# Two attentions on one core: new costs in the plan for Pool, and a copy three steps later

## The chip, the cores and the metric

The kernel runs on one core of a Trainium2 chip. The engines are PE (matrix products), DVE (vector), ACT (activations), POOL (GpSimd) and SP, which issues nearly all DMAs. The metric is the device time of one execution, in microseconds (us), as the median of several runs.

## The reference

For one input `x` (2048 rows of 448 values, 16 heads of 28) two attentions are computed and mixed by a gate.

```python
x = A_x
g = _sigmoid((x * gate_w).sum(-1, keepdims=True))
a = _A_ref(x, A_wqkv, A_wo)
b = _B_ref(x, B_wqkv, B_wo)
return g * a + (1 - g) * b
```

A is a local attention: each row looks at itself and at the seven rows 2, 4, ... 14 places before it, with a softmax over these eight. B is full attention of every row to all 2048. Each has its own projection to queries, keys and values and its own output projection.

## The kernel before

**Stages.** First PE projects `x` to all queries, keys and values (about 250 us). Then come 16 *units* (`NU`), one for each group of four heads and block of 512 queries, each of 16 *steps* (one tile of 128 keys). A step `st` is numbered `16 * unit + tile`, so step 85 is unit 5, tile 5. Last, PE applies the output weights, partly inside units 14 and 15.

**A step.** In `scores` PE makes the score tiles of four heads (three matmuls each, L1022), ACT takes their exponentials (L1025), and PE multiplies the tile before with the values into the bank `av` (L976). Between them PE does up to three matmuls (L144) for the *row maxima* of the unit after the next: DVE reduces these banks to `MX` (L148) and PE needs the banks back. Every 21 or 22 steps one unit's maxima are complete: `max_parts` has ACT write `nmt` and `nmv` (L179, L180) and Pool subtract them (L181, `nmt`); two steps later DVE transposes the result (L186, `nms`) and SP stores it.

**What follows a unit.** While the next unit runs, the result of the last is normalised. `f` is the first step of the next unit, and a tuple gives the steps after it: `fin_copy` (ACT, `osb<-av`, L831) at step 1, `fin_sum` and `fin_sum2` (SP, the row sums out and in again as `fsum`), `fin_inv` (DVE reciprocal L844, Pool `finv` L845), `fin_spread` and `fin_spread2` (SP, `rs<-finv` L849, `rbc<-rs` L854), `fin_on` (Pool, `on<-osb,rbc`, L883), `fin_hi` (ACT, `onhi<-on`, L887), `fin_lo` (Pool, `onlo`, L891), `fin_store` (SP, eight DMAs of 56 KB to `on_hi` and `on_lo`). There is one `osb`.

**Local attention.** It runs on Pool and DVE beside the units, in 8 chunks of channels. For each chunk Pool has eight products of scores (L611, some followed by a half sum, L616), the softmax (L627, L634, L649, L650), eight products with the values (L661) and seven sums (L666); DVE reduces (L621, L632, L642). A planner places them: `item` puts every piece with a cost in us into a list for its engine, and `issue` takes from it, step by step, what is ready by the plan, until the engine's planned lateness `late` would go over a limit (4.2 for Pool). After each step `late` falls by the step's length, 2.25. Work that isn't in the list is added to `late` by hand (`pool_time`). The plan decides in which step's place a piece is written; the engines then run their queues in the order written, and wait only for data. When the lists are empty, `a_done` loads and splits the output weights, with a shift `d` that depends on the step.

Of the kernel before, what the change touches and what calls it, by code (L numbers as in the profile page):

```python
# [20 lines left out]
NU = NG * NB  # L21
# [4 lines left out]
def gated_mix_kernel(ctx: ExitStack, tc: tile.TileContext, xT, xn, gw, wA, wB, woAB, out):  # L26
    nc = tc.nc
# [156 lines left out]
    def max_turn(t):  # L184
        r = sp.tile([128, 32], F32, name="nms")
        nc.vector.transpose(r, t)  # L186
        return r
# [18 lines left out]
    with tc.tile_pool(name="xp", bufs=1) as xp, tc.tile_pool(name="wp", bufs=2) as wp:  # L206
# [203 lines left out]
        r, t = xst[:, 0, 0:3, :], xst[:, 0, 3, :]  # L410
# [40 lines left out]
        for n, t in enumerate(tiles):  # L451
# [4 lines left out]
            for w in splits:  # L456
                i, k = (n - splits[w][0]) * splits[w][1], splits[w][1]
# [36 lines left out]
            if parts and parts[0][0] <= n:  # L494
                _, u, t = parts.pop(0)
                max_store(u, max_turn(t.bitcast(F32)))
            if finished and n < len(tiles) - 3:
                u = finished.pop(0)
# [10 lines left out]
            if n == 70:  # L509
                r = max_turn(omw)  # L510
# [10 lines left out]
    def at(pos, st, f):  # L521
        hooks.setdefault((st, pos), []).append(f)
# [12 lines left out]
    pool = ctx.enter_context(tc.tile_pool(name="psv", bufs=1, space=bass.MemoryType.PSUM))  # L535
# [55 lines left out]
    for nme in ("k", "v"):  # L591
        for i in range(2):
            t = a1.tile([128, HALO + NJ, 56], F32, name=f"{nme}t{i}")
# [3 lines left out]
    def a_load(c, nme):  # L597
        if nme == "q":
            qt[c] = a2.tile([128, NJ, 56], F32, name="qt")
            nc.sync.dma_start(qt[c], a_own[0][c])  # L600
        else:
            t = kvt[nme, c % 2]
            i = 1 if nme == "k" else 2
            nc.sync.dma_start(t[:, 0:HALO, :], a_prev[i][c, :, NJ - HALO:NJ, :])
            nc.sync.dma_start(t[:, HALO:, :], a_own[i][c])

    def a_score(c, w):
        if w == 0:
            Lt[c] = a2.tile([128, W, NJ, 2], F32, name="L", bufs=3)
        p = a3.tile([128, NJ, 56], F32, tag="prod", name="prod")  # L610
        nc.gpsimd.tensor_tensor(out=p, in0=qt[c], in1=kvt["k", c % 2][:, HALO - DIL * w:HALO - DIL * w + NJ, :],  # L611
                                op=ALU.mult)
        prods[c, w] = p.rearrange("p j (h d) -> p (j h) d", d=DH)
        if NR[c, w] == 2:
            lo, hi = prods[c, w][:, :, 0:DH // 2], prods[c, w][:, :, DH // 2:]
            nc.gpsimd.tensor_tensor(out=lo, in0=lo, in1=hi, op=ALU.add)  # L616
            prods[c, w] = lo

    def a_reduce(c, w, i, n):
        r = slice(2 * NJ // n * i, 2 * NJ // n * (i + 1))  # L620
        nc.vector.tensor_reduce(Lt[c][:, w].rearrange("p j h -> p (j h)")[:, r], prods[c, w][:, r], axis=X, op=ALU.add)  # L621
# [56 lines left out]
    def item(eng, key, name, cost, needs, f):  # L678
        lists[eng].append((key, name, cost, needs, f))

    CH, NR = 21, {}
# [4 lines left out]
    for c in range(8):  # L686
        c0 = CH * c
        for nme in "qkv":
            item("sp", c0 if nme != "v" else c0 + 18, ("ld", nme, c), 0,
                 [(("s", c - 2, 7), 3)] if nme != "v" else [(("a", c - 2, 7, 1), 3)],  # L690
                 lambda c=c, nme=nme: a_load(c, nme))
        for w, o in enumerate((0, 2, 5, 8, 11, 14, 17, 20)):
            back = (c, w - 4) if w > 3 else (c - 1, w + 4)
            item("pool", c0 + o, ("s", c, w), 2.05 + 1.0 * (NR[c, w] == 2),
                 [(("ld", "k", c), 4), (("ld", "q", c), 4), (("a", c - 3, 7, 0), 0), (("s", c, w - 1), 0)]
                 + ([(last(*back), 0)] if back in NR else []), lambda c=c, w=w: a_score(c, w))
            for i in range(NR[c, w]):
                item("dve", c0 + o + 2 + 0.1 * i, ("r", c, w, i), 0.32,
                     [(("s", c, w), 3), (("r", c, w, i - 1) if i else last(c, w - 1) if w else ("r",), 0)],
                     lambda c=c, w=w, i=i: a_reduce(c, w, i, NR[c, w]))  # L700
        for i, (eng, o, cost, lag) in enumerate((("pool", 22, 0.68, 2), ("dve", 23, 0.35, 3), ("dve", 23.5, 0.35, 0),
                                                 ("pool", 25, 0.68, 1), ("act", 26, 0.3, 3), ("dve", 27, 0.35, 1),
                                                 ("dve", 27.5, 0.35, 0), ("dve", 27.8, 0.36, 0),
                                                 ("pool", 28, 0.9, 1))):
            item(eng, c0 + o, ("m", c, i), cost, [(last(c, 7) if i == 0 else ("m", c, i - 1), lag)],
                 lambda c=c, i=i: a_softmax(c, i))
        n = 0
        for w in range(W):
            for part in ((0,) if w == 0 else (0, 1)):
                item("pool", c0 + 30 + 1.4 * n, ("a", c, w, part), 1.65 if part == 0 else 2.05,  # L710
                     [(("m", c, 8), 0), (("ld", "v", c), 4),
                      (("a", c, w - 1, 1 if w > 1 else 0) if part == 0 else ("a", c, w, 0), 0)],
                     lambda c=c, w=w, part=part: a_av(c, w, part))
                n += 1
# [3 lines left out]
    late = {"pool": 0.0, "dve": 0.0}  # L718
# [109 lines left out]
    fin = {}  # L828
    def fin_copy(u):
        t = mp.tile([128, 512], F32, name="osb")  # L830
        nc.scalar.activation(t, av, AF.Copy)  # L831
        fin["o"] = t
# [9 lines left out]
    def fin_inv(u):  # L842
        r = sp.tile([128, 16], F32, name="finv")
        nc.vector.reciprocal(r, fin["s"])  # L844
        nc.gpsimd.tensor_tensor(out=r, in0=r, in1=og[:, u % NB, :], op=ALU.mult)  # L845
        fin["rec"] = r
# [50 lines left out]
                r = 112 * g + DH * h  # L897
                dma_r(dst[r:r + DH, 512 * b:512 * b + 512], t[32 * h:32 * h + DH])

    def pool_time(f, *x):  # L900
        late["pool"] += 1.25
        f(*x)


    for u in range(NU - 1):
        f = NJ * (u + 1)
        l = {NU - 3: (1, 2, 5, 6, 9, 12, 13, 15), NU - 2: (1, 2, 5, 6, 8, 10, 10, 12)}.get(
            u, (1, 3, 6, 8, 12, 15, 16, 19))
        at("pre", f + 1, lambda u=u: fin_copy(u))
        at("end", f + l[0], lambda u=u: fin_sum(u))  # L910
        at("end", f + l[1], lambda u=u: fin_sum2(u))
        at("dve", f + l[2], lambda u=u: fin_inv(u))
        at("end", f + l[2], lambda u=u: fin_spread(u))
        at("end", f + l[3], lambda u=u: fin_spread2(u))
        at("end", f + l[4], lambda u=u: pool_time(fin_on, u, fin["r"]))
        at("pre", f + l[5], lambda u=u: fin_hi(u))
        at("end", f + l[6], lambda u=u: pool_time(fin_lo, u, nc.gpsimd))
        at("end", f + l[7], lambda u=u: fin_store(u))


# [20 lines left out]
    part = {}  # L941
# [108 lines left out]
    for u in range(NU):  # L1050
        g, b = divmod(u, NB)
        for kt in range(NJ):
            st = NJ * u + kt
            now[0] = st
            if kt == (8 if u < 12 else 12) and u + 1 < NU:
                load_q(u + 1)
            run("pre", st)
            issue("sp", st, 0)
            if st >= A_START:
                issue("pool", st, 4.2)  # L1060
            if not adone and not any(lists.values()) and st > stored[0]:
                a_done(st)
            cur = {}
            left = s1e - s1c[0]
            for a in scores(u, kt, cur):
                if a == 2:
                    run("mid", st)
            run("dve", st)
            if u and kt == 6:
                late["dve"] += 0.25  # L1070
            if finished:
                v = finished.pop(0)
                t = max_parts(v)
                late["dve"] += 0.3
                turned = {}
                lag = 2 if v < NU - 1 else 1
                at("dve", st + lag, lambda t=t, w=turned: w.update(r=max_turn(t.bitcast(F32))))
                at("end", st + lag, lambda v=v, w=turned: max_store(v, w["r"]))
            issue("dve", st, DLIM)
            issue("act", st, 0)  # L1080
            run("act", st)
            if prev is not None:
                do_av(prev)
            prev = (kt, cur, g)
            if OPS and st >= OPS[0]:
                op_some(st, 7)
            run("end", st)
            step = 2.25 if left else 2.1
            late["dve"] = max(0.0, late["dve"] + 0.58 * min(3, left) - step)
            late["pool"] = max(0.0, late["pool"] - step)  # L1090
            if st == OP0 + 31:
                op_load_b(2, 3)
            if not OPS and s1c[0] == s1e:
                s1_close()
                at("pre", st + 1, lambda: op_t(0))
                at("end", st + 1, lambda: op_split(0))
                OPS.append(st + 2)
# [61 lines left out]
```

## Time and profile before

| | us |
|---|---|
| median of 3 runs (lowest, highest) | 922.4 (921.13, 923.32) |
| profiled execution, its time | 920.4 |
| profiled execution, span of its trace | 918.4 |

In rows of the profile `out<-in` are the program's tile names, `L883` a line of the kernel, `x64` a count, and a bracket such as `[1.18 <-POOL on L883]` the idle time of the engine just before the instruction and what ended it. A row of a table of stretches has the length, the busy time of PE, weight loads, DVE, ACT and POOL, the granted clock of PE, the busy share of the DMA engines and GB/s. A row of the groups has the total busy time and the mean of one in ns. A row of the waits has total, number and longest.

### The profile page before, as it was taken

Reading aid. Unit: us, or ns where it says so; the run is one execution under the profiler, and the core shown is the slowest. Engines: PE = TensorE matmul, PEld = TensorE weight load, DVE = VectorE, ACT = ScalarE, POOL = GpSimd, SP = SyncE. Lnnn points to the kernel's source line nnn. Section 1 sums busy time; section 2 is a strip of 40 time slices with the busy share of each in tenths; the row PEclk is TensorE's granted clock in tenths of the full one; section 3 lists DMA queues with packets and bytes.
Section 4 is the critical chain, followed back from the end, with each engine's and each line's share of the span. In section 5 each row is a group of like instructions: output and inputs, shape, how many; then the busy total and the mean of one; then the engine's idle time right before and its main releaser. Section 6 shows DMA issues by size and latency. Waiting matters only on the chain.

```text
span 918.4 us, 20670 instructions
## 1 busy us (share of the span) xinstructions
PE 905.2 (99%) x8396; PEld 541.2 (59%) x8396; DVE 731.7 (80%) x977; ACT 652.5 (71%) x802; POOL 620.8 (68%) x485
## 2 busy tenths in 40 slices
PE   8999999999999999999999999999999999999998
PEld 6899999999944444444344444343444444466667
DVE  6488999999989999999889999998999888500012
ACT  6456434433388889898788898888989889855551
POOL 2499746554479799998999999999994851300100
PEclk9999999999999999999999999999999999999999
DMA  9977403544374322235135241531412123453422
GB/s 266 294 254 201 127 11 103 154 120 113 81 245 117 86 81 88 69 91 131 33 117 136 81 102 44 140 93 25 111 44 53 34 63 103 147 161 110 138 82 97
DMA packets 101119, 104.30 MB, mean 114 GB/s; under 512 B 61652, under 2 KB 71252, under 8 KB 100240
## 3 DMA queue, kind: packets, MB, share of 16 engines
q1 hardware_dynamic: 100880, 102.72, 39.4%
q8 instruction: 66, 1.08, 0.5%
q10 hardware_dynamic: 144, 0.26, 0.2%
q14 instruction: 29, 0.24, 0.1%
HBM read 61.99 MB, written 40.48 MB: 112 GB/s over the span
## 4 chain that ended last, share of the span: by engine, by line
PE 76%; POOL 12%; SPq 4%; DMA 4%; ACT 2%; DVE 1%; issue 1%; POOLq 0%; ACTq 0%; DVEq 0%
PE T L1022 20%; PE av L976 18%; PE r L298 14%; PE T L815 8%; PE r L293 7%; PE r L144 5%; POOL prod L611 3%; POOL oat L666 3%; POOL prod L661 3%; SPq L101 2%; PE T L144 2%; DMA rbc<-rs 2%; ACT P L1025 1%; SPq L854 1%; DVE MX L148 1%
## 5 line engine op out<-in xcount | busy, mean ns | idle before, releaser
L1025 ACT ACTIVATE P<-T 128x1024 f32<-128x1024 f32 x512 | 497.2, 1024 | 85.2 <-PE T L1022 83.6
L148 DVE TENSOR_REDUCE MX<-T 128x1 f32<-128x512 f32 x470 | 441.1, 954 | 36.0 <-PE T L144 22.5
L976 PE MATMUL av<-P,V 128*32 128x512 f32 x2048 | 273.6, 606 | 0.0
L1022 PEld LDWEIGHTS T<-QH,KH 30*128 30x128 f32 x1024 | 90.9, 182 | 226.8 <-ACT P L1025 203.3
L144 PE MATMUL T<-KH,QP 28*128 28x512 f32 x704 | 219.3, 453 | 1.4 <-DVE MX L148 1.1
L1022 PE MATMUL T<-QH,KH 30*128 30x512 f32 x1024 | 212.0, 489 | 5.9 <-ACT P L1025 5.0
L162 DVE TENSOR_REDUCE MX<-r 128x2 f32<-128x1024 f32 x160 | 192.6, 1221 | 24.6 <-PE r L144 22.9
L1022 PE MATMUL T<-QH,KL 28*128 28x512 f32 x1024 | 186.5, 397 | 0.0
L1022 PE MATMUL T<-QL,KH 28*128 28x512 f32 x1024 | 184.1, 393 | 0.0
L611 POOL TENSOR_TENSOR prod<-qt,kt 128x896 f32<-128x896 f32 x64 | 135.0, 2113 | 1.4 <-DMA kt<-a_scr 1.4
L362 ACT ACTIVATE raw<-r 128x896 f32<-128x896 f32 (+1 forms) x64 | 58.9, 921 | 97.8 <-PE r L298 96.5
L666 POOL TENSOR_TENSOR oat<-oat,prod 128x896 f32<-128x896 f32 x56 | 118.1, 2109 | 2.3
L144 PEld LDWEIGHTS T<-KH,QP 28*128 28x128 f32 x704 | 86.2, 182 | 28.8 <-ACT P L1025 21.4
L661 POOL TENSOR_TENSOR prod<-vt,L 128x896 f32<-128x896 f32 x56 | 95.4, 1703 | 0.6
L363 POOL TENSOR_TENSOR ast<-raw 128x448 f32<-128x448 f32 x48 | 55.5, 1157 | 58.1 <-ACT raw L362 45.6
L1022 PEld LDWEIGHTS T<-QL,KH 28*128 28x128 f32 x1024 | 93.9, 185 | 0.0
L1022 PEld LDWEIGHTS T<-QH,KL 28*128 28x128 f32 x1024 | 92.2, 183 | 1.0
L144 PE MATMUL r<-KH,QP 64*128 64x512 f32 x320 | 86.7, 390 | 0.0
L976 PEld LDWEIGHTS av<-P,V 128*32 128x32 f32 x2048 | 40.3, 108 | 77.5 <-issue 72.4
L298 PE MATMUL r<-wh,xh 64*128 64x448 f32 (+1 forms) x512 | 85.4, 362 | 0.0
L803 DVE TENSOR_TENSOR oalo<-T,oah 128x384 fp32r<-128x384 f32 x16 | 8.9, 557 | 90.8 <-ACT onhi L802 82.2
L298 PE MATMUL r<-wh,xl 64*128 64x448 f32 (+1 forms) x384 | 70.0, 363 | 0.0
(110 smaller groups left out, 1112.9 us busy)
## 6 DMA issues: line engine op xcount, KB each, us to landing
a_scr<-ast SPq DMA_DIRECT2D x24, 448.0 KB
qk_hi<-qkh SPq DMA_DIRECT2D x24, 256.0 KB
qk_lo<-qkh SPq DMA_DIRECT2D x24, 256.0 KB
rbc<-rs SPq DMA_DIRECT2D x60, 64.0 KB
QP<-qk_hi SPq DMA_DIRECT2D x64, 56.0 KB
KL<-qk_lo SPq DMA_DIRECT2D x16, 224.0 KB
QH<-qk_hi SPq DMA_DIRECT2D x64, 56.0 KB
QL<-qk_lo SPq DMA_DIRECT2D x64, 56.0 KB
```

The costliest lines, as they stand in the source:

```text
L144: nc.tensor.matmul(bank, qhis[u][h % 2][r, 128 * qs:128 * qs + 128], KH[u // NB % 3][r, 512 * kc:512 * kc + 512], start=True, stop=True)
L148: r = nc.vector.tensor_reduce(MX[:, n % NMX:n % NMX + k], bank, axis=X, op=ALU.max)
L162: nc.vector.tensor_reduce(m, PM[k], axis=X, op=ALU.max)
L293: nc.tensor.matmul(bank, ws[c][rows, k, t[4]:t[4] + 128], x, start=first, stop=last)
L298: nc.tensor.matmul(bank[:, 0:cols], x, ws[c][rows, k, 0:cols], start=first, stop=last)
L611: nc.gpsimd.tensor_tensor(out=p, in0=qt[c], in1=kvt["k", c % 2][:, HALO - DIL * w:HALO - DIL * w + NJ, :], op=ALU.mult)
L661: nc.gpsimd.tensor_tensor(out=dst.rearrange("p j (h d) -> p j h d", d=DH), in0=kvt["v", c % 2][:, HALO - DIL * w:HALO - DIL * w + NJ, :].r ...
L666: nc.gpsimd.tensor_tensor(out=oat[c], in0=oat[c], in1=oat[c, w], op=ALU.add)
L815: writes(bank, nc.tensor.matmul(bank[:, :D], src, wo[c][:, k, :], start=(first and k == ks[0] and i == 0), stop=(last and k == ks[-1] and ...
L976: nc.tensor.matmul(av[32 * h:32 * h + 32, :], V[:, kt, 4 * g + h, :], tiles_[h], start=(kt == 0), stop=(kt == NJ - 1), skip_group_check=True)
L1022: nc.tensor.matmul(bank[a], (KH[g % 3], KH[g % 3], KL[g % 2])[t][r, ks], (qh, ql, qh)[t][r, :], start=(t == 0), stop=(t == 2))
L1025: e = nc.scalar.activation(p, RP[0] if a == "2" else mine, AF.Exp, scale=SCALE).ins
```

## The change

The costs that the plan knows for Pool are set to other values, and Pool's two small instructions outside the list, `finv` and `nmt`, are added to `late` with 0.18 each. For units 0 to 10 `fin_hi`, `fin_lo` and `fin_store` come at steps 18, 19 and 22 of their count instead of 15, 16 and 19.

```diff
-            item("pool", c0 + o, ("s", c, w), 2.05 + 1.0 * (NR[c, w] == 2),
+            item("pool", c0 + o, ("s", c, w), 2.15 + 0.98 * (NR[c, w] == 2),
...
-        for i, (eng, o, cost, lag) in enumerate((("pool", 22, 0.68, 2), ("dve", 23, 0.35, 3), ("dve", 23.5, 0.35, 0),
-                                                 ("pool", 25, 0.68, 1), ("act", 26, 0.3, 3), ("dve", 27, 0.35, 1),
+        for i, (eng, o, cost, lag) in enumerate((("pool", 22, 0.69, 2), ("dve", 23, 0.35, 3), ("dve", 23.5, 0.35, 0),
+                                                 ("pool", 25, 0.69, 1), ("act", 26, 0.3, 3), ("dve", 27, 0.35, 1),
                                                  ("dve", 27.5, 0.35, 0), ("dve", 27.8, 0.36, 0),
-                                                 ("pool", 28, 0.9, 1))):
+                                                 ("pool", 28, 1.14, 1))):
...
-                item("pool", c0 + 30 + 1.4 * n, ("a", c, w, part), 1.65 if part == 0 else 2.05,
+                item("pool", c0 + 30 + 1.4 * n, ("a", c, w, part), 1.72 if part == 0 else 2.08,
...
-    def pool_time(f, *x):
-        late["pool"] += 1.25
+    def pool_time(t, f, *x):
+        late["pool"] += t
         f(*x)
...
         l = {NU - 3: (1, 2, 5, 6, 9, 12, 13, 15), NU - 2: (1, 2, 5, 6, 8, 10, 10, 12)}.get(
-            u, (1, 3, 6, 8, 12, 15, 16, 19))
+            u, (1, 3, 6, 8, 12, 18, 19, 22) if u < NU - 5 else (1, 3, 6, 8, 12, 15, 16, 19))
...
-        at("dve", f + l[2], lambda u=u: fin_inv(u))
+        at("dve", f + l[2], lambda u=u: pool_time(0.18, fin_inv, u))
...
-        at("end", f + l[4], lambda u=u: pool_time(fin_on, u, fin["r"]))
+        at("end", f + l[4], lambda u=u: pool_time(1.24, fin_on, u, fin["r"]))
...
-        at("end", f + l[6], lambda u=u: pool_time(fin_lo, u, nc.gpsimd))
+        at("end", f + l[6], lambda u=u: pool_time(1.24, fin_lo, u, nc.gpsimd))
...
                 late["dve"] += 0.3
+                late["pool"] += 0.18
```

What it moves shows in the order of the instructions. First Pool in unit 5, around the `nmt` of step 85 and the `finv` of step 86; `prod` is a product of local attention, `oat` its sum. Before:

```order
L666 TENSOR_TENSOR oat<-oat,prod_5715 128x896
L661 TENSOR_TENSOR prod_5802<-vt_3321,L 128x896
L611 TENSOR_TENSOR prod<-qt,kt_3320 128x896
L616 TENSOR_TENSOR prod<-prod 128x32x14
L181 TENSOR_TENSOR nmt<-nmv,nmt 128x16
L666 TENSOR_TENSOR oat<-oat,prod_5802 128x896
L845 TENSOR_TENSOR finv<-finv,og 128x16
```

And in the change, from the `onlo` of the unit before on:

```order
L891 TENSOR_TENSOR onlo<-on,onhi 128x512
L661 TENSOR_TENSOR prod_5791<-vt_3321,L 128x896
L666 TENSOR_TENSOR oat<-oat,prod_5791 128x896
L181 TENSOR_TENSOR nmt<-nmv,nmt 128x16
L661 TENSOR_TENSOR prod_5853<-vt_3321,L 128x896
L845 TENSOR_TENSOR finv<-finv,og 128x16
```

The product L611 with its half sum L616 and one L661 that stood ahead of `nmt` now come behind it, and `onlo` stands closer to it.

Second SP's queue of DMAs in unit 5 (`rs_4_72` are the row sums, `rs_4_88` their inverses). Before:

```order
L101 DMA on_hi<-onhi 28x512 x4
L101 DMA on_lo<-onlo 28x512 x4
L840 DMA fsum<-rs_4_72 128x16
L101 DMA QP_155<-qk_hi 28x512
L101 DMA QP_156<-qk_hi 28x512
L101 DMA QP_155<-qk_hi 28x512
L101 DMA QP_156<-qk_hi 28x512
L849 DMA rs_4_88<-finv 128x16
```

And in the change, up to `rbc`, which before had the loads of `qt` and `kt` ahead of it:

```order
L101 DMA QP_155<-qk_hi 28x512
L101 DMA QP_156<-qk_hi 28x512
L101 DMA on_hi<-onhi 28x512 x4
L101 DMA on_lo<-onlo 28x512 x4
L849 DMA rs_4_88<-finv 128x16
L191 DMA nm_108<-nms 32x32 x4
L101 DMA QH<-qk_hi 28x512 x4
L101 DMA QL<-qk_lo 28x512 x4
L101 DMA QH<-nm_106 4x512 x2
L854 DMA rbc<-rs_4_88 32x512 x4
L600 DMA qt<-a_scr_61 128x896
```

The eight stores went from ahead of `fsum` to just ahead of `rs<-finv`, and `qt` went behind `rbc`.

Third ACT at the end of a unit (two exponentials are one step). Before:

```order
L887 ACTIVATE onhi<-on 128x512
L1025 ACTIVATE P_3300<-T_3279 128x1024
L1025 ACTIVATE P_3301<-T_3275 128x1024
L1025 ACTIVATE P_3294<-T_3279 128x1024
L1025 ACTIVATE P_3295<-T_3271 128x1024
L831 ACTIVATE osb<-av 128x512
```

And in the change:

```order
L831 ACTIVATE osb<-av 128x512
L1025 ACTIVATE P_3296<-T_3279 128x1024
L1025 ACTIVATE P_3297<-T_3275 128x1024
L887 ACTIVATE onhi<-on 128x512
L1025 ACTIVATE P_3298<-T_3279 128x1024
```

The copy stood ahead of the last step's exponentials and two steps ahead of `osb<-av`; now it comes one step after it.

In the plan as a whole the last sum of local attention is placed at step 215 instead of 212; `a_done` comes at step 220 instead of 217, with `d` 0 instead of 3. PE's rows are the same in both but for the number of one buffer.

## The prediction

> **What bounds the kernel now.** I read the page first, then the stretch in which the change acts.
>
> ```profile
> span 918.4 us, 20670 instructions
> PE 905.2 (99%) x8396; PEld 541.2 (59%) x8396; DVE 731.7 (80%) x977; ACT 652.5 (71%) x802; POOL 620.8 (68%) x485
> PE 76%; POOL 12%; SPq 4%; DMA 4%; ACT 2%; DVE 1%; issue 1%; POOLq 0%; ACTq 0%; DVEq 0%
> 253.00:695.10 442.10, 435.33 (x4411) 180.62 (x4409) 416.08 (x625) 385.54 (x432) 417.15 (x288) 1.00 0.35 95
> 659.10:695.10 36.00, 36.00 (x375) 15.01 (x371) 33.83 (x49) 31.84 (x35) 35.37 (x24) 1.00 0.15 39
> 434.30:474.90 40.60, 38.41 (x368) 15.61 (x368) 34.97 (x53) 32.13 (x37) 39.14 (x25) 0.96 0.24 70
> ```
>
> The first three rows are of the page (the third is the share of the chain of waits by engine), the others of the table of stretches (length, then busy time of PE, PEld, DVE, ACT, POOL, then granted clock and DMA). PE sets the time. In the 442.10 us of units 0 to 11 it is idle 6.8 us, and Pool, 68% of the span, is busy 417 of the 442. A unit of 16 steps that nothing disturbs, unit 11, takes 36.00 us, so a step takes 2.25 us; unit 5 takes 40.60. What the change can win is what such units lose. I asked for stretches around each place where PE's starts lie apart:
>
> ```profile
> 430.00:436.00 6.00, 5.29 (x58) 1.93 (x54) 5.09 (x9) 5.10 (x6) 4.47 (x5) 1.00 0.72 159
> 454.00:464.00 10.00, 8.22 (x67) 3.06 (x61) 7.32 (x14) 5.26 (x6) 9.92 (x8) 0.83 0.18 46
> 472.00:477.00 5.00, 4.55 (x50) 1.87 (x46) 4.16 (x7) 4.26 (x6) 4.97 (x3) 1.00 0.00 0
> 581.00:587.00 6.00, 4.78 (x50) 1.83 (x46) 4.60 (x8) 4.68 (x7) 4.93 (x3) 1.00 0.46 178
> 603.00:608.00 5.00, 4.88 (x53) 1.92 (x49) 4.74 (x10) 4.05 (x5) 4.84 (x7) 1.00 0.02 2
> 618.00:625.00 7.00, 5.45 (x58) 1.98 (x54) 5.25 (x9) 5.34 (x7) 7.00 (x5) 1.00 0.07 22
> ```
>
> Who is waited for there, from the waits of ACT, DVE and POOL in 252 to 695 us (total, times, longest):
>
> ```profile
> ACT onhi L887 <- POOL on L883: 4.0, 4, 1.5
> DVE nms L186 <- POOL nmt L181: 2.7, 2, 2.5
> POOL on L883 <- DMA rbc<-rs: 7.1, 3, 4.2
> 583.31 0.63 ACT L887 ACTIVATE onhi<-on 128x512 fp32r<-128x512 f32 x1 [1.18 <-POOL on L883]
> 455.23 0.21 DVE L186 STREAM_TRANSPOSE nms<-nmt 128x32 f32<-128x32 f32 x1 [2.47 <-POOL nmt L181]
> 603.46 0.21 DVE L186 STREAM_TRANSPOSE nms<-nmt 128x32 f32<-128x32 f32 x1 [0.26 <-POOL nmt L181]
> ```
>
> Both causes are a Pool that runs behind the steps for which the list planned it. **A:** four times, at the last step of a unit, ACT holds its exponentials because `fin_hi` stands ahead of them in its queue and Pool's `on` isn't done. Those are the stretches at 430, 472, 581 and 618 us: PE idles 0.71 + 0.45 + 1.22 + 1.55 = 3.9 us. **B:** twice DVE waits for Pool's tiny `nmt`, with the maxima of the banks that PE needs queued behind it, at 454 and 603 us: PE idles 1.78 + 0.12 us, and after the first its clock is 0.83 over 10 us, another 1.7: together 3.6.
>
> [...]
>
> **The change, part by part.** *The copy three steps later.* For units 0 to 10 `fin_hi` goes from step 15 to 18 of its count, that is from the last step of a unit to step 2 of the next, `fin_lo` and `fin_store` with it. `on` stays. The worst wait so far is 1.5 us; three steps are 6.8 us. What reads late next is `fin_copy` of the next unit at step 1, which overwrites `osb` that `on` reads; that is two steps, 4.5 us, later than the old place, still 3 us more than the worst wait. A goes: -3.9 us.
>
> Price on ACT: the copy now follows one step after `fin_copy` instead of two before it.
>
> ```profile
> 657.47 0.63 ACT L887 ACTIVATE onhi<-on 128x512 fp32r<-128x512 f32 x1
> 657.99 1.94 ACT L1025 ACTIVATE P<-T 128x1024 f32<-128x1024 f32 x2
> 660.09 1.94 ACT L1025 ACTIVATE P<-T 128x1024 f32<-128x1024 f32 x2 [0.16 <-PE T L1022]
> 661.92 0.60 ACT L831 ACTIVATE osb<-av 128x512 f32<-128x512 f32 x1
> ```
>
> Each lies in the gap that ACT has per step (2.25 less 1.94 of exponentials) and overruns it by some 0.3 us; after the copy ACT still waits 0.16 for PE in the next step, and unit 11, with both, takes 36.00. In adjacent steps the overrun could reach 0.3 us for PE in 11 units, 3.3 us; nothing is the other end, and I take nothing.
>
> *The store on SP.* Its eight DMAs now stand right ahead of `rs<-finv` instead of ahead of `fsum`, as the second excerpt shows.
>
> ```profile
> 416.46 0.22 POOL L845 TENSOR_TENSOR finv<-finv,og 128x16 f32<-128x16 f32 x1
> 416.70 0.34 SPq L849 DMA_DIRECT2D rs<-finv  x1
> 423.39 1.75 SPq L854 DMA_DIRECT2D rbc<-rs  x4
> 431.37 1.29 POOL L883 TENSOR_TENSOR on<-osb,rbc 128x512 f32<-128x512 f32 x1 [4.21 <-DMA rbc<-rs]
> 465.20 0.43 SPq L605 DMA_DIRECT2D kt<-a_scr  x1
> ```
>
> SP waits for `finv` anyway. Four issues take 1.7 us, eight 3.5; the first four need only `onhi`. Between `onlo` and `finv` Pool now has, by the first excerpt, two products (1.70), one sum (2.11) and `nmt`, 5.7 us, so the eight are out before `finv` comes: nothing. If that cover were gone, `rbc` would come up to 3.5 us later. In unit 5 three loads (`qt` and `kt`, 1.3 us of issues up to 465.2) leave the way between `rs` and `rbc`: a small gain that I don't count.
>
> *The list.* Local attention costs a little more in the plan, and `finv` and `nmt` are counted, so less is put into each step: the last sum is placed at step 215 instead of 212. Ahead of each `nmt` stands less Pool work. Its unit prices, and how late `nmt` is behind ACT's `nmv`:
>
> ```profile
> L611 POOL TENSOR_TENSOR prod<-qt,kt 128x896 f32<-128x896 f32 x64 | 135.0, 2113 | 1.4 <-DMA kt<-a_scr 1.4
> L666 POOL TENSOR_TENSOR oat<-oat,prod 128x896 f32<-128x896 f32 x48 | 101.2, 2109 | 1.9
> L661 POOL TENSOR_TENSOR prod<-vt,L 128x896 f32<-128x896 f32 x49 | 83.5, 1703 | 0.6
> L616 POOL TENSOR_TENSOR prod<-prod 128x448 f32<-128x448 f32 x40 | 41.0, 1025 | 3.1
> 448.62 0.22 ACT L180 ACTIVATE nmv<-m 128x16 f32<-128x16 f32 x1
> 454.98 0.22 POOL L181 TENSOR_TENSOR nmt<-nmv,nmt 128x16 fp32r<-128x16 f32 x1
> 599.24 0.22 ACT L180 ACTIVATE nmv<-m 128x16 f32<-128x16 f32 x1
> 603.21 0.22 POOL L181 TENSOR_TENSOR nmt<-nmv,nmt 128x16 fp32r<-128x16 f32 x1
> 695.91 0.24 ACT L180 ACTIVATE nmv<-m 128x16 f32<-128x16 f32 x1
> 697.68 0.21 POOL L181 TENSOR_TENSOR nmt<-nmv,nmt 128x16 fp32r<-128x16 f32 x1
> ```
>
> `nmt` is behind by 6.4 us at step 85 (DVE waits 2.47), 4.0 at step 149 (0.26), 1.8 at step 191 (none): DVE waits from about 3.8 us. Counting Pool's rows from the `nmt` of step 21 to that of step 85, the change has one L611, one L616 and one L661 fewer: 4.8 us. Up to step 149 it has three L611 and two L616 fewer, 8.4 us; up to step 191, one L661 and two L666 (and a small one), 6.7. Against that PE no longer pauses and lets Pool catch up: by then 0.7, 5.9 and 7.5 us of A and B are gone. New lag: 6.4 - 4.8 + 0.7 = 2.3 at step 85; 4.0 - 8.4 + 5.9 = 1.5 at 149; 1.8 - 6.7 + 7.5 = 2.6 at 191. All are under 3.8, with 1.2 us to spare. B goes: -3.6. This holds if Pool's waits for `rbc` (7.1 us before) don't grow by more than that spare; a Pool with less in its queue reaches `on` earlier and finds `rbc` no sooner, so they may.
>
> *The tail.* Local attention ends three steps later, but Pool has room there:
>
> ```profile
> 711.50 0.23 POOL L845 TENSOR_TENSOR finv<-finv,og 128x16 f32<-128x16 f32 x1 [11.66 <-DVE finv L844]
> ```
>
> Weights and output start at the steps they had: `a_done` comes at step 220 instead of 217, but its shift `d` falls from 3 to 0. PE's rows are the same but for a buffer's number. Cost nothing; if the last store were late, the first output loads would be, a step or two.
>
> **Sum.** The profiled execution took 920.4 us (span 918.4): 920.4 - 3.9 - 3.6 = 912.9. The median of the runs, 922.4, lies 2.0 above it, so 914.9.
>
> **Rivals.** *One `nmt` still late.* Pool idles longer for `rbc` in units 4 and 5 than the spare of 1.2 us, and the `nmt` of step 106 or 127 stops DVE once. For: the wait was 4.2 us with 14.7 us from `finv` to `on`, and that way isn't shortened in unit 4. Against: unit 5's loads leave the way. Price up to that of step 85, 1.8 + 1.7: up to 918.4, about 917.
>
> *The stores delay `rbc`.* The eight transfers (448 KB) ahead of `rs` push `rbc` back by 448 KB at the 205 GB/s seen in the next row, 2.2 us, in the three units where Pool was waiting: 6.6 us of Pool, less 1.2 spare, 5.4 us back: 920.3.
>
> ```profile
> 463.00:468.00 5.00, 5.00 (x54) 2.25 (x53) 5.00 (x9) 4.45 (x5) 4.92 (x5) 1.00 0.65 205
> ```
>
> [...] No row here shows these stores and `rs` close together.
>
> *The list does nothing, only the copy counts.* The costs of the large pieces go up by 1 to 5%, and the limit per step (4.2) may leave Pool as full as it was: A alone goes, 922.4 - 3.9 = 918.5. Against: the counted rows.
>
> *Slower.* The waits of B multiply: without A's pauses Pool, busy 417 of 442 us, never catches up, and the four `nmt` at steps 106, 127, 170 and 191 each cost what step 85 did, 3.5 us: 914.9 + 14 = 928.9. It decides from a lag of about 6 us at each of them, 3.5 more than I work out.
>
> **How the numbers follow.** Forecast 0.45 (own range 913.4 to 916.5), one `nmt` late 0.25, stores 0.12, copy alone 0.12, slower 0.06. The likeliest gives 914.9. The low end takes in all that units 4 to 9 lose against six times 36.00 us, 225.6 - 216.0 = 9.6, by the sum row of their six stretches: 922.4 - 9.6 = 912.8.
>
> ```profile
> sum 225.60, PE 219.78 PEld 90.81 DVE 210.72 ACT 193.63 POOL 215.33; mean PE 36.63 PEld 15.13 DVE 35.12 ACT 32.27 POOL 35.89
> ```
>
> The high end holds the second and fourth case and part of the third, 919.8; some 0.15 stays outside. A measurement can tell about 0.2% (1.8 us) from no change: faster takes the first, second and fourth case and half of the third, 0.88; same the other half, 0.06; slower 0.06.
>
> **What would show it.** The wait of `onhi` for `on` at 0, no stretch of 10 us with PE's clock under 1 in the middle, units 4 to 9 at 36 us each, and the `nms` wait at 0 say that both steps held. An `onhi` wait left means that two steps of slack weren't enough; a wait of `nms` in units 6 to 11, that Pool's ledger was off; waits of `on` for `rbc` well over 7.1 us, that the stores stand in the way; 0.3 us more in step 2 of each unit, that ACT pays for the copy's place.

## The result and the profile after

The changed kernel takes 913.86 us (median of 5 runs, 912.73 to 914.36) against 922.64 us (921.13 to 923.32): ratio 0.9904, 95% interval 0.989 to 0.9919. The forecast was 914.9 us. The profiled execution took 912.73 us, 7.7 less than the one before. Its page, rows in the order in which the prediction showed those of before (span, busy time by engine, the chain of waits by engine):

```profile
span 911.0 us, 20699 instructions
PE 903.8 (99%) x8396; PEld 536.3 (59%) x8396; DVE 731.7 (80%) x977; ACT 652.2 (72%) x802; POOL 620.6 (68%) x485
PE 95%; DMA 1%; ACT 1%; SPq 1%; DVE 0%; issue 0%; POOL 0%; ACTq 0%; DVEq 0%; POOLq 0%
```

Pool does the same work, 620.6 us against 620.8, but its share of the chain went from 12% to 0. What bounds the kernel is now PE alone. Where the time came from is in the table of stretches (length, busy time of PE, PEld, DVE, ACT, POOL, granted clock, DMA share and GB/s): units 0 to 11, then unit 5, then unit 11.

```profile
252.60:687.50 434.90, 433.69 (x4411) 180.42 (x4410) 416.33 (x625) 385.08 (x431) 411.51 (x284) 1.00 0.35 97
433.90:470.10 36.20, 36.20 (x372) 15.04 (x369) 34.68 (x54) 32.00 (x37) 35.49 (x25) 1.00 0.26 78
651.00:687.50 36.50, 36.37 (x374) 15.07 (x370) 34.86 (x53) 32.29 (x36) 35.58 (x24) 1.00 0.22 51
```

Units 0 to 11 went from 442.4 us (unit 0 of the kernel before starts at 252.69; the prediction's row begins 0.3 us later) to 434.9, which is all of what the span lost. PE's idle time there went from 6.8 to 1.2 us. Unit 5, which took 40.60, takes 36.20; but unit 11, which nothing had disturbed (36.00), now takes 36.50. Who still waits, in the waits of ACT, DVE and POOL from 252 to 690 us (total, times, longest):

```profile
ACT P L1025 <- PE T L1022: 48.4, 155, 0.5
ACT raw L362 <- PE r L298: 1.7, 1, 1.7
...
DVE MX L148 <- PE T L144: 9.9, 34, 0.6
DVE MX L148 <- PE T L1022: 2.6, 14, 0.2
DVE MX L162 <- PE r L144: 0.2, 1, 0.2
...
POOL on L883 <- DMA rbc<-rs: 2.3, 2, 1.4
```

The list of ACT is whole, and so is that of DVE: the four waits of `onhi` for `on` and the two of `nms` for `nmt` are gone. Pool waits 2.3 us for `rbc` instead of 7.1.

### The profile page after: what moved, and what is told of

Read it like the earlier page. It is cut to its first block, busy times and chain, and to the rows that moved or that the text cites. A ratio compares the mean times of both kernels' runs of the same rounds, so it can differ in the third digit from the quotient of the medians.

```text
span 911.0 us, 20699 instructions
## 1 busy us (share of the span) xinstructions
PE 903.8 (99%) x8396; PEld 536.3 (59%) x8396; DVE 731.7 (80%) x977; ACT 652.2 (72%) x802; POOL 620.6 (68%) x485
## 4 chain that ended last, share of the span: by engine, by line
PE 95%; DMA 1%; ACT 1%; SPq 1%; DVE 0%; issue 0%; POOL 0%; ACTq 0%; DVEq 0%; POOLq 0%
PE T L1022 29%; PE av L976 27%; PE r L298 15%; PE T L815 8%; PE r L293 7%; PE r L144 4%; PE T L144 4%; ACT P L1025 1%; PE T L793 1%; DMA V<-in_xT 1%; DMA onlo<-on_lo 1%; SPq L101 0%; DMA rs<-finv 0%; SPq L854 0%; ACT wo L758 0%
## 5 line engine op out<-in xcount | busy, mean ns | idle before, releaser
L611 POOL TENSOR_TENSOR prod<-qt,kt 128x896 f32<-128x896 f32 x64 | 135.1, 2114 | 1.8 <-DMA kt<-a_scr 1.8
L661 POOL TENSOR_TENSOR prod<-vt,L 128x896 f32<-128x896 f32 x56 | 95.4, 1704 | 0.4
L298 PE MATMUL r<-wh,xh 64*128 64x448 f32 (+1 forms) x512 | 83.5, 362 | 0.0
L144 PE MATMUL r<-KH,QP 64*128 64x512 f32 x320 | 83.1, 390 | 0.0
```

What stands on the lines that cost most here:

```text
L144: nc.tensor.matmul(bank, qhis[u][h % 2][r, 128 * qs:128 * qs + 128], KH[u // NB % 3][r, 512 * kc:512 * kc + 512], start=True, stop=True)
L298: nc.tensor.matmul(bank[:, 0:cols], x, ws[c][rows, k, 0:cols], start=first, stop=last)
L661: nc.gpsimd.tensor_tensor(out=dst.rearrange("p j (h d) -> p j h d", d=DH), in0=kvt["v", c % 2][:, HALO - DIL * w:HALO - DIL * w + NJ, :].r ...
```

## The experiments

Two theories stood against each other. By the *theory of the sum*, the prediction's, the two parts of the change remove two separate losses: the later copy removes A (ACT waits for Pool's `on`), the new list removes B (DVE waits for Pool's `nmt`). By the rival, *one cause*, both losses are one late Pool: the list alone cures both, and the copy alone lets B grow, since the pauses of A were what let Pool catch up.

### Each part alone

The copy alone is the kernel before with one line of the change:

```diff
-            u, (1, 3, 6, 8, 12, 15, 16, 19))
+            u, (1, 3, 6, 8, 12, 18, 19, 22) if u < NU - 5 else (1, 3, 6, 8, 12, 15, 16, 19))
```

> The copy, its subtraction and its store three steps later, with the plan's costs as they were before. Theory of the sum (the waits of ACT for on, A, and of DVE for nmt, B, are two separate losses): A goes, B stays, 922.6 - 3.9 = 918.7 us; no wait of onhi for on, waits of nms for nmt 2.7 us as before. Rival, one cause (both are a late Pool, and A's pauses were what let it catch up): A goes, but Pool now stays late and nmt is waited for more often or longer, well over 2.7 us in all; 919.5 to 922.6 us.

Measured: 919.62 us (918.06 to 923.72) against 922.32, ratio 0.9979 [0.9967, 0.9992]. The costs alone are the change without that line:

```diff
-            u, (1, 3, 6, 8, 12, 18, 19, 22) if u < NU - 5 else (1, 3, 6, 8, 12, 15, 16, 19))
+            u, (1, 3, 6, 8, 12, 15, 16, 19))
```

> All the plan's new costs, the two small instructions counted, but the copy, its subtraction and its store at steps 15, 16 and 19 as before. Theory of the sum: B goes, A stays, 922.6 - 3.6 = 919.0 us; onhi waits for on 4 us in all. Rival, one cause: with less in Pool's queue on is done in time too, so A goes as well, onhi waits under 0.5 us; 914 to 915.5 us, like the change.

Measured: 913.42 us (912.03 to 913.67), ratio 0.9907 [0.9894, 0.992]. In time of the kernel before on that chip, the interval of the copy alone is 919.3 to 921.6 and that of the costs alone 912.5 to 914.9. The sum's 918.7 and 919.0 lie outside them; the rival's ranges, 919.5 to 922.6 and 914 to 915.5, overlap them. The waits of the copy alone:

```profile
DVE nms L186 <- POOL nmt L181: 4.4, 2, 3.1
POOL on L883 <- DMA rbc<-rs: 5.7, 3, 3.4
```

and its units 6 and 9, in the table of stretches:

```profile
470.20:511.20 41.00, 38.57 (x375) 15.50 (x371) 35.03 (x55) 32.27 (x38) 40.45 (x28) 0.96 0.38 92
583.40:621.00 37.60, 36.65 (x375) 15.06 (x371) 35.28 (x55) 32.39 (x38) 36.82 (x26) 1.00 0.28 76
```

A is gone (no `onhi` row), as its step said. But `nms` now waits 4.4 us where it waited 2.7, and the first wait comes one unit later, at step 106, with Pool busy 40.45 of unit 6's 41.00 us. ACT's `nmv` and Pool's `nmt` of that step, first before the change, then with the copy alone:

```profile
500.65 0.20 ACT L180 ACTIVATE nmv<-m 128x16 f32<-128x16 f32 x1
504.17 0.22 POOL L181 TENSOR_TENSOR nmt<-nmv,nmt 128x16 fp32r<-128x16 f32 x1
```

```profile
496.43 0.20 ACT L180 ACTIVATE nmv<-m 128x16 f32<-128x16 f32 x1
503.35 0.22 POOL L181 TENSOR_TENSOR nmt<-nmv,nmt 128x16 fp32r<-128x16 f32 x1
```

Pool comes at nearly the same time, 0.8 us earlier, after the same 230.7 us of work since unit 0 began; ACT comes 4.2 us earlier, so that `nmt` is now 6.9 us behind instead of 3.5. The copy moves the place where a late Pool stops PE; it gives Pool no time. Not all of it is as the rival said: of the pauses that are gone by step 106, A's two are 1.2 us, and the larger one is B's own stall at step 85 (3.5 us with the slow clock). That stall is gone because Pool waited 0.2 us for `rbc` in unit 4 instead of 4.2 and came to `nmt` in time. The copy's own price isn't what is missing of the 3.9 us: without units 6 and 9, units 3 to 11 take 253.1 us with the copy alone and 253.1 with the list alone, a run that follows. The waits of ACT with the costs alone, where the copy stands at its old place:

```profile
ACT P L1025 <- PE T L1022: 49.2, 155, 1.7
ACT raw L362 <- PE r L298: 1.7, 1, 1.7
```

No `onhi` row here either: with less put into each step, Pool's `on` is done before ACT reaches the copy. DVE has no `nms` row. The list cures both.

### Which entries of the list

The change raises the costs of the large pieces and also counts two small instructions, `finv` and `nmt`, at 0.18. The list alone leaves both the copy and the small ones as they were. Against the change it has the old line of the copy, as above, and:

```diff
-        at("dve", f + l[2], lambda u=u: pool_time(0.18, fin_inv, u))
+        at("dve", f + l[2], lambda u=u: fin_inv(u))
...
-                late["pool"] += 0.18
```

> The new costs of the local attention's pieces alone; finv and nmt not counted, the copy where it was. Some 20 small instructions of 0.22 us are 4.4 us of Pool over 175 steps, a tenth of the Pool work that the new costs push back. If the pieces' costs carry the change: within 1 us of the run with all costs. If counting the small ones is needed: nmt is late again at step 85 or 149, 1 to 4 us above it.

Measured: 912.25 us (912.13 to 913.25), ratio 0.99 [0.9887, 0.9913]: the whole gain, without the small ones. The same kernel and the change itself, side by side on another chip:

> The pieces' costs alone (finv and nmt not counted, the copy where it was) again, for a comparison with the change on the same chip. If the later copy costs anything where it isn't needed (units 3 to 11 of the change took 36.24 us on average, here 36.14): 0.5 to 1.5 us under the change. If not: the same within 0.5 us.

> The change itself beside the others on this chip. 912.5 to 914.5 us.

Measured: the list alone 912.59 us (911.99 to 914.42), ratio 0.9899 [0.9884, 0.9914]; the change 913.24 us (912.94 to 914.49), ratio 0.9906 [0.9892, 0.9921]; both against 921.47. By times alone the two can't be told apart. The small ones by themselves, added to the kernel before:

```diff
+        at("dve", f + l[2], lambda u=u: pool_time(0.18, fin_inv, u))
...
+                late["pool"] += 0.18
```

> Only finv and nmt counted, with 0.18 us each; the pieces' costs and the copy as before. Ahead of the nmt of step 85 that takes about eight small ones, 1.5 to 2 us, out of Pool's queue, of the 2.5 us by which it was late. If they are a small part of one cause: waits of nms and of onhi shorter but there, 918 to 921 us. If counting them is what matters: 913 to 915 us.

Measured: 918.12 us (916.89 to 920.6) against 921.03, ratio 0.9968 [0.9955, 0.9982]. Its waits of ACT, DVE and POOL show both losses still there, at fewer places each:

```profile
ACT onhi L887 <- POOL on L883: 2.7, 2, 2.5
...
DVE nms L186 <- POOL nmt L181: 2.2, 1, 2.2
POOL on L883 <- DMA rbc<-rs: 4.9, 2, 3.4
```

And half the rise of the large costs, with small ones and copy as before (costs that differ by 0.01 keep their new values):

```diff
-            item("pool", c0 + o, ("s", c, w), 2.05 + 1.0 * (NR[c, w] == 2),
+            item("pool", c0 + o, ("s", c, w), 2.10 + 0.99 * (NR[c, w] == 2),
...
-                                                 ("pool", 28, 0.9, 1))):
+                                                 ("pool", 28, 1.02, 1))):
...
-                item("pool", c0 + 30 + 1.4 * n, ("a", c, w, part), 1.65 if part == 0 else 2.05,
+                item("pool", c0 + 30 + 1.4 * n, ("a", c, w, part), 1.685 if part == 0 else 2.065,
```

> Half of the rise of the pieces' costs (2.10 + 0.99, 1.685, 2.065, 1.02), nothing else changed, copy where it was. If the gain follows the lateness of Pool piece by piece: about half of it, 917 us, with waits of onhi for on and of nms for nmt of 1 to 4 us left. If it is a matter of a margin (nothing is lost once on and nmt come in time): nearly all, 912.5 to 914.5 us. If even half leaves nmt of step 85 late: one wait of nms, 916 to 919 us.

Measured: 913.9 us (912.6 to 914.36), ratio 0.9914 [0.9899, 0.9929]. Half the rise brings 7.1 us by the medians, the whole 10.1 and 8.9 on the two other chips, and the intervals of all three overlap: the costs act as a margin. Once Pool is a little ahead nothing more is won: units 3 to 11 take 325.3 us with half the rise and 325.3 to 325.4 with the whole. The traces say the same more sharply. This table has Pool's busy time from the start of unit 0 up to the `nmt` of steps 85 and 149, and how far that `nmt` is behind ACT's `nmv`, in us:

| | Pool's work up to step 85 | `nmt` behind | up to step 149 | `nmt` behind |
|---|---|---|---|---|
| before | 183.4 | 6.4 | 326.8 | 4.0 |
| copy alone | 183.6 | 3.9 | 326.8 | 5.1 |
| small ones alone | 183.4 | 6.1 | 323.7 | 0.3 |
| half the rise | 180.4 | 0.6 | 321.7 | 1.6 |
| list alone | 180.5 | 1.0 | 318.8 | 0.3 |
| the change | 178.8 | 2.0 | 318.7 | 0.3 |

Where DVE waited (from about 3.8 us) and where it didn't follows these columns. The copy alone takes nothing out of Pool's way. The small ones alone take nothing out ahead of step 85, against what was expected of them, and that stall stays; they take 3.1 us out ahead of step 149, and that one goes. Half the rise takes out 3.0 and 5.1 us, and both go.

### The copy's place and the stores

The prediction's rival on the stores said that eight DMAs on SP ahead of a small one that Pool needs would delay Pool. The change puts them ahead of `rs`. Two steps later still, at steps 20, 21 and 24, they come ahead of `rbc` instead:

```diff
-            u, (1, 3, 6, 8, 12, 18, 19, 22) if u < NU - 5 else (1, 3, 6, 8, 12, 15, 16, 19))
+            u, (1, 3, 6, 8, 12, 20, 21, 24) if u < NU - 5 else (1, 3, 6, 8, 12, 15, 16, 19))
```

> The change, with the copy, its subtraction and its store two steps later still (20, 21, 24 instead of 18, 19, 22), so that it isn't in the step right after the copy of av. If ACT pays for two such copies in adjacent steps, as units of 36.1 to 36.5 us after the change (36.0 undisturbed before) suggest: units 3 to 11 0.1 to 0.2 us shorter each, 912.5 to 913 against the change's 913.9. If not: 913.9, within 0.5. Against both: the store now stands just ahead of rbc's four issues; if that delays on, Pool waits for rbc more than 2.3 us and time rises by 1 to 3 us.

Measured: 926.59 us (924.47 to 928.43), ratio 1.0051 [1.0035, 1.0066]: slower than the kernel before, by far the largest miss of these expectations. Its waits of POOL and DVE, and then the place in the trace at which one of those for `rbc` ends (start, duration, engine and line):

```profile
POOL on L883 <- DMA rbc<-rs: 19.2, 7, 4.6
DVE nms L186 <- POOL nmt L181: 5.7, 3, 2.6
```

```profile
504.90 3.50 SPq L101 DMA_DIRECT2D on_hi<-onhi  x4
508.44 1.69 SPq L101 DMA_DIRECT2D on_lo<-onlo  x4
510.18 1.75 SPq L854 DMA_DIRECT2D rbc<-rs  x4
...
513.97 1.28 POOL L883 TENSOR_TENSOR on<-osb,rbc 128x512 f32<-128x512 f32 x1 [3.98 <-DMA rbc<-rs]
```

SP's issues come one after the other, in the order of its queue: the eight stores keep it from 504.90 to 510.13 us, the four of `rbc` follow from 510.18, and Pool stands 3.98 us. To know whether this is the copy or the stores, the stores alone were put there, copy as in the change:

```diff
-            u, (1, 3, 6, 8, 12, 18, 19, 22) if u < NU - 5 else (1, 3, 6, 8, 12, 15, 16, 19))
+            u, (1, 3, 6, 8, 12, 18, 19, 24) if u < NU - 5 else (1, 3, 6, 8, 12, 15, 16, 19))
```

> The change with fin_store alone two steps later, step 24 instead of 22, so that the eight stores are issued between finv's write-out and rbc's four issues. If the stores ahead of rbc are what made the run with the copy at 20 slow (Pool waited 19.2 us for rbc there): rbc comes eight issues, 3.5 us, later in ten units, Pool waits 15 to 25 us for it, nmt is late in units 5 to 9, 920 to 928 us. If the later copy itself was the cause (ACT, or Pool's order): like the change, 913 to 915 us, waits for rbc under 4 us.

Measured: 925.76 us (922.85 to 928.94) against 921.47, ratio 1.0042 [1.0027, 1.0057]. And the late copy with the stores one step later, behind `rbc`:

```diff
-            u, (1, 3, 6, 8, 12, 18, 19, 22) if u < NU - 5 else (1, 3, 6, 8, 12, 15, 16, 19))
+            u, (1, 3, 6, 8, 12, 20, 21, 25) if u < NU - 5 else (1, 3, 6, 8, 12, 15, 16, 19))
```

> The copy two steps later than in the change (20, 21) and the store at 25, behind rbc in SP's queue. Theory of the stores: Pool's waits for rbc back at 1 to 4 us and no wait of nms for nmt, 912.5 to 914 us; and if ACT pays for a copy in the step after the copy of av, units 3 to 11 a little shorter than the change's. If the later copy was the cause: 920 to 928 us as before.

Measured: 914.24 us (912.57 to 915.63), ratio 0.9911 [0.9893, 0.9929]. The waits of the two, first the stores alone ahead of `rbc`:

```profile
POOL on L883 <- DMA rbc<-rs: 15.7, 6, 4.5
DVE nms L186 <- POOL nmt L181: 6.5, 4, 2.0
```

then the late copy with the stores behind `rbc`, of which this and one wait of 0.3 us for `rbc` are Pool's only ones at `on`:

```profile
POOL on L883 <- DMA on_lo<-onlo: 0.8, 2, 0.5
```

It is the stores: against the change on the same chip (913.24) they cost 12.5 us ahead of `rbc`, while with the copy later still and the stores behind `rbc` the time is 1.0 us from it. And it is SP's issuing, not the transfers: in the two runs with the stores ahead of `rbc` Pool waits for `rbc` 13 times, and in 11 of them `on` starts 1.6 to 2.0 us after SP has issued the last part of `rbc` (3.3 and 2.8 us in the others). In the three waits of the kernel before it was 4.5 to 6.2. So `rbc` isn't slower behind the stores; it is issued later, by the 3.4 to 5.3 us that the eight issues take (why they take more than 3.4 at some places isn't shown).

The last run of this kind takes the list alone and puts only its stores behind `rbc`:

```diff
-            u, (1, 3, 6, 8, 12, 15, 16, 19))
+            u, (1, 3, 6, 8, 12, 15, 16, 25) if u < NU - 5 else (1, 3, 6, 8, 12, 15, 16, 19))
```

> The pieces' costs alone, copy at 15, but the store at 25, behind rbc in SP's queue instead of ahead of fsum. If the stores also delay fsum or finv where they stood: Pool's waits for rbc (1.9 us in the run without this) go and time falls by up to 0.5 us. If not: the same as the pieces' costs alone, 912 to 913 us.

Measured: 912.59 us (912.2 to 914.54) against 921.03, ratio 0.9906 [0.9891, 0.9921], the same as the list alone. Pool's waits for `rbc` do go, but that is worth nothing here. Of the places tried, the stores matter only right ahead of `rbc`.

### What the copy's new place costs

The times are too coarse for it, the traces are not: outside the start of unit 0 they repeat to 0.1 us. Units 3 to 11 of the change, and of the costs alone, which differ only in the copy's line:

```profile
361.30:687.50 326.20, 325.94 (x3318) 135.40 (x3314) 313.49 (x476) 289.72 (x325) 317.34 (x211) 1.00 0.34 89
```

```profile
363.00:688.30 325.30, 325.19 (x3316) 135.00 (x3312) 312.13 (x472) 289.68 (x325) 311.63 (x208) 1.00 0.34 89
```

0.9 us, 0.1 per unit on average. The second trace of the change has 326.1, the three of the list alone (one with its stores behind `rbc`) 325.3, 325.4 and 325.4, half the rise 325.3. No unit of these has a wait of `onhi` or `nms`. By position in the unit, the step after the copy's is the longer one: step 3 takes 2.33 us on average in units 3 to 11 of the change and 2.26 with the list alone. With the copy at step 20, which is step 4 of the unit, and the stores behind `rbc`, step 5 is the longer one (2.31, against 2.23), and units 3 to 11 take 325.9 us. So most of the price comes with the copy wherever it stands early in a unit, and about 0.2 us with its place right after `osb<-av`; by what, through ACT or otherwise, isn't shown. It isn't even over the units: the change takes about 0.2 us more than the list alone in units 4, 6, 9 and 11 and nothing more in unit 5. So with the list in place the copy's move costs 0.8 to 0.9 us and brings nothing; the list alone is the better kernel by that, though the difference in the medians on one chip, 913.24 less 912.59, is within both ranges.

## Why the prediction was right, and where it was not

**The bound and the sum: right in size, in part by luck.** Pool's lateness was put at A + B = 7.5 us, and 7.4 us of span are gone. But units 4 to 9, where all of it was looked for, went from 225.6 to 217.2 us, 8.5 less: A and B were 1 us too small. The other units gave back about 1, of which the prediction had nothing, most of it in units 3 and 11. The two errors cancel in the trace. The measured median is 1.0 us under the forecast.

**"A goes: -3.9 us", by the copy three steps later: right size, wrong cause.** This is the step that failed. With the copy alone A goes too, but the time falls by 2.7 us and not by 3.9, since the waits of B grow from 2.7 to 4.4 us (by its interval, 0.7 to 3.0 us are gained). With the costs alone A goes without the copy. A and B were added as two losses, each with a part of the change to its name, though the prediction itself had said that both were one late Pool, and its ledger even counted the pauses of A as time in which Pool catches up. Followed through, that sentence says that a pause which goes, A's or B's, feeds the next wait for `nmt`. The sum came out right only because the list removes the whole.

**"Price on ACT ... I take nothing": mis-sized.** It is 0.8 to 0.9 us in nine units, between the 0 taken and the bound of 3.3. The sign, 0.3 us more in step 2 of each unit, isn't seen: step 2 is as long as with the list alone, and step 3 is 0.07 us longer. The 0.5 us of unit 11 isn't the copy's alone: that unit takes 36.28 to 36.31 with the list alone and 36.04 with the copy alone.

**The ledger of the list: held.** `nmv` and the `nmt` behind it at steps 85, 149 and 191 of the change:

```profile
448.23 0.21 ACT L180 ACTIVATE nmv<-m 128x16 f32<-128x16 f32 x1
450.23 0.22 POOL L181 TENSOR_TENSOR nmt<-nmv,nmt 128x16 fp32r<-128x16 f32 x1
592.79 0.21 ACT L180 ACTIVATE nmv<-m 128x16 f32<-128x16 f32 x1
593.09 0.22 POOL L181 TENSOR_TENSOR nmt<-nmv,nmt 128x16 fp32r<-128x16 f32 x1
688.32 0.20 ACT L180 ACTIVATE nmv<-m 128x16 f32<-128x16 f32 x1
689.23 0.23 POOL L181 TENSOR_TENSOR nmt<-nmv,nmt 128x16 fp32r<-128x16 f32 x1
```

The lags are 2.0, 0.3 and 0.9 us, forecast 2.3, 1.5 and 2.6. The work taken out ahead of them is 4.6, 8.1 and 6.4 us by Pool's busy time, where 4.8, 8.4 and 6.7 were counted. The last two came out shorter because Pool also stands idle 1.9 and 2.0 us less ahead of them: its waits for `rbc`, feared to grow, fell from 7.1 to 2.3 us in all.

**The clock.** B was sized at 3.6 us, 1.7 of it by the row that showed the clock at 0.83 over 10 us. That was right for this stall: PE's clock is at 0.50 from 458.38 to 461.79 us, which costs 1.7; the longest gap in the 3.41 us ahead of it was 1.2 us. It isn't so for every stall: with the small ones alone PE stood 2.5 us at one go, at 472 us, and the clock stayed at 1.00.

**The stores: cover held, and the rival had a point.** In unit 5 of the change they go out from 446.26 to 449.61 us, and `rs` with `finv` follows at 452.32, after a pause:

```profile
446.26 1.63 SPq L101 DMA_DIRECT2D on_hi<-onhi  x4
447.99 1.62 SPq L101 DMA_DIRECT2D on_lo<-onlo  x4
452.32 0.35 SPq L849 DMA_DIRECT2D rs<-finv  x1
```

Nothing, as taken. Two steps later in SP's queue the same eight cost 12 us and turn the gain into a loss. The rival had the right stores, but neither the place, which is ahead of `rbc`, nor the mechanism: it went by 448 KB of transfers, 2.2 us, and what delays `rbc` is the 3.4 to 5.3 us in which SP issues the eight. The transfers of the stores aren't seen to cost anything here: behind them `on` starts 1.6 to 2.0 us after the last issue of `rbc` in 11 of 13 waits, no later than the 4.5 to 6.2 us of the kernel before.

**The other rivals.** *Only the copy counts, the list does nothing* fell by the opposite: only the list counts. *One `nmt` still late* didn't come. *Slower, B multiplies* is what the copy would have led to without the list, at a smaller price: two late `nmt` as before, the first of them later and longer, not four more, and the time fell all the same. The tail cost nothing: units 12 and 13 take 36.03 and 35.98 us, with 36.03 and 36.00 before.

## What to carry to other kernels

When two stalls have one late engine behind them, they are one loss: removing a stall on the waiting side takes away the pause in which the late engine caught up, and some of the loss comes back at its next consumer, here 1.2 of 3.9 us by the medians. Ask of every edit whether it gives the late engine time or only moves the place where its lateness is felt; only the first can be booked as a gain by itself. And a group of transfers that is moved along SP's queue was priced by what stood right behind it: the eight stores were free ahead of `rs` and cost 12.5 us ahead of `rbc`.

## What the runs showed of the hardware that was not expected

Where PE's clock fell within the units of these traces, it was 0.50 for 3.41 us, and the idle time of PE ahead of it doesn't tell alone whether it falls. In the run with the copy at steps 20, 21 and 24 it did so three times within units 5 to 9. Two of these stretches, with the 3.41 us ahead of each:

```profile
454.91:458.32 3.41, 2.12 (x17) 0.53 (x13) 2.19 (x5) 1.78 (x2) 3.41 (x5) 1.00 0.00 0
458.32:461.73 3.41, 3.34 (x18) 1.04 (x18) 1.84 (x3) 1.94 (x2) 3.33 (x3) 0.50 0.20 44
516.35:519.76 3.41, 2.13 (x17) 0.53 (x13) 2.41 (x5) 1.82 (x2) 3.41 (x3) 1.00 0.01 2
519.76:523.17 3.41, 3.36 (x18) 1.04 (x18) 2.40 (x4) 1.94 (x2) 3.33 (x3) 0.50 0.00 0
```

The starts, 458.32, 519.76 and 615.33, are 61.44 and 95.57 us apart, 18 and 28 times 3.413 us. PE was idle 1.29, 1.28 and 1.33 us of the stretch ahead. In the kernel before the next fall of the clock, at 919.18 us, 0.7 us behind the last instruction, comes 135.0 times 3.413 us after the start of its slow stretch. So the others are taken here as windows of that length, counted in each trace from such a fall; that their borders lie there is an estimate from these distances. Windows of the kernel before:

```profile
454.97:458.38 3.41, 1.63 (x15) 0.68 (x13) 3.15 (x7) 0.74 (x2) 3.41 (x5) 1.00 0.02 2
458.38:461.79 3.41, 3.41 (x25) 1.38 (x23) 2.33 (x4) 1.61 (x2) 3.33 (x3) 0.50 0.22 48
581.26:584.67 3.41, 2.42 (x27) 0.94 (x23) 3.00 (x6) 2.23 (x3) 2.68 (x2) 1.00 0.76 297
618.81:622.22 3.41, 2.66 (x27) 0.94 (x23) 3.22 (x6) 1.90 (x4) 3.41 (x3) 1.00 0.02 5
622.22:625.63 3.41, 2.61 (x26) 1.15 (x28) 1.85 (x3) 3.26 (x4) 3.33 (x3) 1.00 0.02 5
```

1.78 us idle was followed by half speed; 0.99, 0.75 and 0.80 were not. The last two are halves of one stall of 1.55 us that, so counted, lies across a border. With the small ones alone, counted from the fall of the clock at the end of its trace, a stall of 2.50 us lies across one too:

```profile
469.76:473.17 3.41, 2.33 (x27) 0.90 (x23) 2.73 (x5) 0.94 (x2) 1.93 (x3) 1.00 0.03 7
473.17:476.58 3.41, 1.99 (x23) 0.89 (x23) 1.24 (x2) 3.25 (x5) 3.41 (x2) 1.00 0.00 0
```

Its halves are 1.08 and 1.42 us, and no half speed followed. So of eight such windows within the units of all the traces with 1.28 us or more of idle time seven were followed by half speed and this one wasn't; at 0.93 to 1.08 us four were (all at the start of unit 0) and four weren't. B's 1.7 us of clock thus wasn't certain from the length of the stall; what else decides isn't shown. The start of unit 0 is a case in between: in four of the profiled executions (costs alone, the second of the list alone, and both with the copy at step 20) its second step ran at a clock of 0.50 for 3.41 us and the unit took 37.8 to 38.0 us instead of 36.45, which is why spans of single profiles are compared here from unit 3 on.
